# Last products of one feed-forward layer set between the first products of the next, and token sums moved to VectorE

## The chip, the cores and the metric

The program runs on one core of one Trainium2 chip. Times are device microseconds (us) from the first to the last instruction of one execution, lower is better. The core has a matrix engine (TensorE, PE in the rows; PEld is its weight load), three elementwise engines (VectorE = DVE, ScalarE = ACT, GpSimd = POOL) and SyncE (SP), whose queue issues almost every DMA here. Matmul results stand in PSUM banks, everything else in SBUF, tensors in DRAM.

## The reference, cut to what matters

```python
def reference(q, k, v, M_prev, z_prev, beta, moe_w_in, moe_w_out, moe2_w_in, moe2_w_out):
    attn = attention(q, k, v, M_prev, z_prev, beta)   # 4 batches, 8 heads, 576 tokens, 64 wide
    x = attn.transpose(0, 2, 1, 3).reshape(2304, 512)
    h = x @ moe_w_in                # 512 x 2048
    x = (h * cos(h)) @ moe_w_out    # 2048 x 512
    h = x @ moe2_w_in
    return (h * tanh(log1p(exp(h)))) @ moe2_w_out
```

All of it is float32 with zero tolerance for a single rounded pass, so the kernel splits each operand into a high part (the value rounded to the matmul's input format) and a low part (the rest), and makes three matmuls for each product: high by high, high by low, low by high.

## The kernel before, in words

The program has three parts, written one behind the other and laid out by a framework that orders the instructions of each engine itself; `tc.issue_after(mark)` holds what is written under it back until a marked instruction has been issued. `TURNS` is a table that says which engine makes a helper's pass: "v" is VectorE, "p" GpSimd, "a" ScalarE, and "vp" alternates.

**Attention and the first feed-forward layer.** `ffn` works on token blocks and units of the hidden width. `first(k)` makes the unit's hidden values (L422), an elementwise chain turns them into `g`, and `second(k)`, two units behind, multiplies `g` by w_out into the output banks `y` (L481). The hidden width is done in two halves; the first runs beside attention, the second (`m2`) on four blocks of 512 tokens and a last block of 256 tokens. That last block has four units, 96 matmuls of 256 columns for `first` and 96 for `second`. `fin_full` fetches a block's partial result from the first half (L503), adds it (L504) and stores the sum to `ysF` (L505).

**The second feed-forward layer** (`strassen_ffn`) uses Strassen's seven products in place of eight. It works on three token blocks of 768 tokens, eight groups for each. A group makes seven `product`s (A11, S2, A12, S3, S1, A22, S4, in this order), each of six matmuls of 384 columns (L630) into three PSUM banks. Between them stand the four `unit`s of the group before, nine matmuls of 512 columns each (L663). After a product, `add` (L644, VectorE) adds a bank to a value in SBUF; the Mish function runs on ScalarE (L648), the high part is cast on ScalarE (L125) and the low part taken by subtraction (L651, "ml"). Banks A and B are reused within a group: the product S3 goes on in the bank of S2 and can't start before the `add` that reads S2, nor A22 before the add that reads S3. A group needs the sums of the weights (`wq`, L601, from `wsD`) and of the tokens (`xc`).

**Token sums.** `strassen_x` fetches a token block's four quarters b11, b12, b21, b22 from `ysF` (`xr`, L565) and forms seven operands as high part (L571, ScalarE) and low part (L572, "x3l"): A11 = b11, t1 = b12 - b11 (L579), S2 = t2 = b22 - t1 (L579), A12 = b21, S3 = b22 - b12 (L589), S1 = t1, A22 = b21 - t2 (L594), S4 = b22. For the first block this runs while `ffn` still has its large blocks, and the operands are stored to `xsD` (L574); `load_sums` fetches them again (L609) with the first group's weights. For the second and third block it runs between the last group of the block before and the first of its own, straight into the operands.

The second layer's w_out is split piece by piece (`gc`): fetched to `wst`, two passes on ScalarE (L125, L140), two on VectorE (L141, L142), a cast and a low part (L553).

Of the kernel before, what the change touches and what calls it, by code (L numbers as in the profile page):

```python
# [9 lines left out]
F32 = mybir.dt.float32  # L10
# [4 lines left out]
ALU = mybir.AluOpType  # L15
# [11 lines left out]
AHEAD = 3  # L27
XSUM0 = 37
CONVR = 0.9
PACE1 = 1.5  # L30
# [6 lines left out]
    sc="p", ws="p", w0l="pv", w1l="vp", w2l="vp", w3l="vp", gl="p", gh="v", bh="a", mh="a",  # L37
    wh="ap", aT="av", yl="p", ml="vp", y0="v", y1="a", aD="v", y3="a", x3l="pv", x3d="v", ws4="p", ws2="a", wh2="a",
)
# [7 lines left out]
def attention_moe_moe_kernel(  # L47
# [14 lines left out]
    nc = tc.nc  # L62
    P = 128
# [4 lines left out]
    DFF = w1i.shape[1]  # L68
# [10 lines left out]
    xsH = tc.dram_tile([NP, P, NT], F32, name="xsH")  # L79
# [36 lines left out]
    def turn_of(kind, first=False):  # L116
        kind += "0" if first else ""
        n = counts.get(kind, 0)
        counts[kind] = n + 1
        return {"a": nc.scalar, "p": nc.gpsimd, "v": nc.vector}[TURNS[kind][n % len(TURNS[kind])]]  # L120
# [244 lines left out]
    marks = {}  # L365
# [35 lines left out]

    def ffn(pools, seq, weights, elem, load_x, mm2, finish, ready=lambda blk: True):

# [24 lines left out]

        def second(k):
            blk, half, f, n, fst, lst = seq[k]  # L430
            if fst:
                i = seq_blocks.index(blk)
                ys[blk] = [pools[i % len(pools)].tile([P, SM], F32, tag="y", name="y", bufs=BUFS["y"])
                           for _ in range(NC * blk[1] // SM)]
            gH, gL = gs.pop(k)
            T = blk[1]
            for a in range(n):
                tl, fa = (f + a) // 2, (f + a) % 2
                g = (gH[:, a * T:(a + 1) * T], gL[:, a * T:(a + 1) * T])
                mm2(ys[blk], g, weights[half][tl], fa, T, fst and a == 0, lst and a == n - 1)  # L440
            if lst:
                finish(blk, ys.pop(blk))

        seq_blocks = sorted({u[0] for u in seq})
        n = len(seq)
        for k in range(0, n + 2, 2):
            for j in (k, k + 1):
                if j < n:
                    nb = seq[min(j + NTL, n - 1)][0]
                    first(j)  # L450
                    if nb not in xs and ready(nb):
                        xs[nb] = load_x(nb)
                    yield "m1", j
            for j in (k - 2, k - 1):
                if 0 <= j < n:
                    second(j)
                    yield "m2", j
# [26 lines left out]
    def part(ys_, blk, i):  # L484

        t0, T = blk
        per = SM // T
        return ys_[:, i * per:(i + 1) * per, t0:t0 + T]
# [69 lines left out]
    def strassen_x(t0, out, store=False):  # L558
# [10 lines left out]
        def halves(n, x):  # L569
            d = wk.tile([P, 2, 2, TS], F32R, tag="xc" + u, name="xc", bufs=BUFS["xc" + u])  # L570
            nc.scalar.activation(d[:, 0], x, AF.Copy)  # L571
            turn_of("x3l").tensor_tensor(d[:, 1], x, d[:, 0].bitcast(F32), ALU.subtract)  # L572
            if store:
                nc.sync.dma_start(xsD[SLOT[n]], d.rearrange("p l c t -> p (l c t)").bitcast(F32))  # L574
            out[n] = d
# [12 lines left out]
        yield  # L588
        nc.gpsimd.tensor_tensor(b12, b22, b12, ALU.subtract)  # L589
        halves("S3", b12)  # L590
        yield
        halves("S1", t1)
        yield
        nc.gpsimd.tensor_tensor(b21, b21, t2, ALU.subtract)  # L594
        halves("A22", b21)
# [22 lines left out]

    def strassen_ffn(pool, wo, xs, w):

# [34 lines left out]
        def unit(k, g, half, f, last):  # L655
# [9 lines left out]
            if tl == ng - 1 and last:  # L665
                for t, b in enumerate(ys.pop((t0, half))):
# [3 lines left out]
                    nc.sync.dma_start(out[r:r + P, :], o)  # L670

        n = len(groups)
        g = {}
        for k in range(n + 1):
            if k < n:
# [7 lines left out]
                u2 = add(B, x1)  # L683
            if k > 0:
                unit(k - 1, g.pop((k - 1, 0, 0)), 0, 0, 0)
            if k < n:
# [3 lines left out]
                u3 = add(B, x1)  # L690
            if k > 0:
                unit(k - 1, g.pop((k - 1, 1, 1)), 1, 1, 0)
            if k < n:
# [6 lines left out]
                g[k, 1, 0] = act(c21, c21)  # L700
            if k > 0:
                unit(k - 1, g.pop((k - 1, 1, 0)), 0, 1, 1)
            if k < n:
# [5 lines left out]
                if groups[k][1] == ng - 2 and k + 2 < n:  # L709
# [3 lines left out]
                    with behind():  # L713
                        next(coming)
            if k > 0:
                unit(k - 1, g.pop((k - 1, 0, 1)), 1, 0, 1)
            yield k
# [60 lines left out]
    wo2, gc = strassen_weights(w2i, w2o)  # L778
    m2 = ffn(b_pools, seq2, {1: w_b}, elem_cos("bh"), load_block(xsH, xsL, True), mm2_t, fin_full)
    gx = strassen_x(0, {}, True)  # L780
    xs, w0 = {0: {}}, {}
    gl = load_sums(xs[0], w0)
    with tc.issue_after(marks["sp"]):
        i = made_c = 0
        while True:
# [11 lines left out]
            if i >= XSUM0 and i % 4 == 3:  # L797
                with tc.issue_after(marks["cos"]), tc.issue_after(last_sin[0]):
                    next(gx, None)
            if large[-2] in marks:  # L800
                drain(gx)
                with tc.issue_after(marks[large[-2]]):
                    next(gl, None)
    with tc.issue_after(marks[large[-2]]):
        drain(gl)
    with tc.issue_after(last_sin[0]):
        table = nc.scalar.preload_act_table_set("mish").ins
    with tc.issue_after(table), tc.issue_after(marks[large[-2]]):
        for k in strassen_ffn(b_pools[0], wo2, xs, w0):
            while made_c < min(2 * k + 4, DFF // P):  # L810
                with behind():
                    made_c = next(gc)
# [65 lines left out]
```

## Time and profile before

| | us |
|---|---|
| median of 3 runs (1068.15 to 1069.03) | 1068.41 |
| the profiled execution, its own time | 1070.39 |
| its span, first to last instruction | 1068.6 |
| PE busy in it (97%) | 1031.4 |
| DVE busy (52%) | 559.0 |
| ACT busy (50%) | 532.5 |
| POOL busy (39%) | 417.5 |
| granted TensorE clock, mean | 0.984 |

The shares are means over the whole span. Attention fills the first part up to about 560 us, the first layer's second half runs alone to 661, the second layer from there to the end. The stretches that the change touches are 634 to 704 us (the way from one layer to the next), 785 to 811 and 917 to 930 us (the token sums of the second and third token block).

### The profile page before, as it was taken

What the parts mean: (1) busy time and instruction counts of PE and PEld (TensorE: products, weight loads), DVE (VectorE), ACT (ScalarE), POOL (GpSimd) and SP (SyncE); (2) the same over time, 40 slices, a digit from 0 to 9 for tenths busy, and PEclk for the clock granted to TensorE, in tenths of its full rate; (3) what the DMA queues carried; (4) which work ended last, traced back from release to release, by engine and by line L of the source; (5) the groups of instructions that cost most, each with busy time, mean ns of one, the idle gap of its engine ahead of it and who ended that gap; (6) DMA issues with size and microseconds to landing.
All of it is one profiled execution on the core that took longest, in us unless ns stands there. A gap on an engine that the chain in (4) does not pass through costs nothing. (4 is left out here: it accounts for less than half of the span.)

```text
span 1068.6 us, 18074 instructions
## 1 busy us (share of the span) xinstructions
PE 1031.4 (97%) x6560; PEld 888.7 (83%) x6560; DVE 559.0 (52%) x1224; ACT 532.5 (50%) x1154; POOL 417.5 (39%) x407
## 2 busy tenths in 40 slices
PE   6988999999999999999999999899989999999998
PEld 4756778787878899998888889789878998898997
DVE  3689865555554537785756756435563222522221
ACT  5887675546464633425635656435544322442323
POOL 3379734323232324654656774212243111611111
PEclk7998999999999999999999999999989999999999
DMA  7477432423231165333688776975645344563431
GB/s 261 132 226 244 154 97 90 131 63 122 68 98 36 63 247 170 99 108 120 238 303 296 297 274 245 410 269 169 187 144 175 117 117 130 167 187 110 120 98 59
DMA packets 88712, 177.36 MB, mean 166 GB/s; under 512 B 8240, under 2 KB 29232, under 8 KB 87600
## 3 DMA queue, kind: packets, MB, share of 16 engines
q1 hardware_dynamic: 88624, 176.21, 49.8%
q8 instruction: 52, 0.85, 0.3%
q14 instruction: 36, 0.29, 0.1%
HBM read 132.40 MB, written 43.78 MB: 165 GB/s over the span
## 5 line engine op out<-in xcount | busy, mean ns | idle before, releaser
L481 PE MATMUL y<-g,w 128*128 128x256 f32 (+1 forms) x1344 | 219.8, 317 | 4.2 <-ACT aT L125 4.2
L663 PE MATMUL y<-wo,g 128*128 128x512 f32 x864 | 217.6, 394 | 0.0
L481 PEld LDWEIGHTS y<-g,w 128*128 128x128 f32 x1344 | 191.0, 190 | 29.5 <-issue 9.1
L630 PE MATMUL h<-xc,wq 128*128 128x384 f32 x1008 | 199.0, 341 | 8.7 <-DVE us L644 4.9
L422 PE MATMUL h<-xbH,w 128*128 128x256 f32 (+1 forms) x896 | 206.5, 317 | 0.0
L630 PEld LDWEIGHTS h<-xc,wq 128*128 128x128 f32 x1008 | 181.5, 190 | 19.9 <-DVE us L644 7.1
L663 PEld LDWEIGHTS y<-wo,g 128*128 128x128 f32 x864 | 162.0, 189 | 28.6
L651 POOL TENSOR_TENSOR g<-us,g 128x384 fp32r<-128x384 f32 x48 | 51.9, 1080 | 289.1 <-ACT g L125 282.1
L422 PEld LDWEIGHTS h<-xbH,w 128*128 128x128 f32 x896 | 150.9, 191 | 12.3 <-issue 0.7
L644 DVE TENSOR_TENSOR us<-h,us 128x384 f32<-128x384 f32 x120 | 66.7, 556 | 175.1 <-PE h L630 174.5
L274 POOL TENSOR_SCALAR at<-at,sm,omg 128x128 f32<-128x128 f32 (+2 forms) x144 | 102.6, 722 | 131.3 <-DVE sm L272 95.3
L394 POOL TENSOR_TENSOR g<-u,g 128x512 fp32r<-128x512 f32 x72 | 105.5, 1481 | 123.8 <-DVE g L127 45.1
L422 PE MATMUL h<-xbL,w 128*128 128x256 f32 (+1 forms) x448 | 141.0, 315 | 0.0
L422 PEld LDWEIGHTS h<-xbL,w 128*128 128x128 f32 x448 | 85.7, 191 | 5.4 <-issue 0.3
L376 ACT ACTIVATE u<-h 128x512 int32<-128x512 f32 x72 | 42.6, 594 | 93.2 <-PE h L422 84.5
L648 ACT ACTIVATE us<-us 128x384 f32<-128x384 f32 x72 | 37.7, 524 | 102.0 <-DVE us L644 99.4
L252 ACT ACTIVATE at<-at,mn 128x128 f32<-128x128 f32 (+3 forms) x128 | 71.0, 556 | 28.5 <-DVE mn L249 24.2
L142 DVE SCALAR_TENSOR_TENSOR wst<-wst 128x512 int32<-128x512 int32 x64 | 72.4, 1142 | 0.6
L377 DVE SCALAR_TENSOR_TENSOR u<-u,h 128x512 f32<-128x512 int32 x72 | 48.7, 681 | 43.5 <-ACT u L376 43.1
L306 PE MATMUL tp<-ident,at 128*128 128x128 f32 x384 | 64.1, 288 | 6.5 <-DVE xL L338 3.0
L333 PE MATMUL o<-aT,vt 128*64 128x128 f32 (+1 forms) x896 | 67.4, 276 | 2.0 <-ACT aT L125 2.0
L249 DVE CUSTOM_DVE_ANT_0 at<-sp,mask 128x128 f32<-128x128 f32 (+3 forms) x128 | 59.1, 482 | 19.4 <-PE sp L247 11.8
(99 smaller groups left out, 1289.3 us busy)
## 6 DMA issues: line engine op xcount, KB each, us to landing
wq<-wsD SPq DMA_DIRECT2D x168, 256.0 KB, 2.9
wsD<-ws SPq DMA_DIRECT2D x8, 1792.0 KB, 8.3
wst<-in_w1i_dram SPq DMA_DIRECT2D x16, 512.0 KB, 4.4
wst<-in_w1o_dram SPq DMA_DIRECT2D x16, 512.0 KB, 4.4
wst<-in_w2i_dram SPq DMA_DIRECT2D x16, 512.0 KB, 4.7
wst<-in_w2o_dram SPq DMA_DIRECT2D x16, 512.0 KB, 4.7
xsD<-xc SPq DMA_DIRECT2D x7, 768.0 KB, 4.5
xc<-xsD SPq DMA_DIRECT2D x7, 768.0 KB, 9.0
```

The lines of the kernel that those rows point to most:

```text
L142: nc.vector.scalar_tensor_tensor(lo, hi, 3, lo, ALU.logical_shift_left, ALU.bitwise_or)
L249: nc.vector.tensor_tensor_reduce(at[:, :N], sp[:, :N], mask[:, SM - q0:SM - q0 + N], SSC, 3.0e38, ALU.add, ALU.min, mn[:, j:j + 1])
L252: marks["act"] = nc.scalar.activation(at[:, :N], at[:, :N], AF.Exp, bias=mn[:, j:j + 1], scale=-1.0, accum_out=sm[:, j:j + 1]).ins
L274: turn_of("sc", b == 0).tensor_scalar(at[:, :N], at[:, :N], sm[:, j:j + 1], gates[j], ALU.mult, ALU.mult)
L306: nc.tensor.transpose(tp[:, c:c + P], at[:, c:c + P], ident)
L333: marks["pe"] = nc.tensor.matmul(o[j * D:(j + 1) * D, :n], st["vt"][:kk, c, j * D:(j + 1) * D], a, start=False, stop=c == i, skip_group_ch ...
L394: turn_of(kind).tensor_tensor(gL, g, gH.bitcast(F32), ALU.subtract)
L422: nc.tensor.matmul(h[:, a * T:(a + 1) * T], w_[:, c, f0:f0 + P], x_[c], start=m == 0, stop=m == 3 * NC - 1)
L481: nc.tensor.matmul(y[e // per][:, cols], w_[:, f, es], g_, start=fst and m == 0 and e % per == 0, stop=lst and m == 2, skip_group_check=True)
L630: nc.tensor.matmul(b, w[:, wl, c], x[:, xl, c], start=first and m == 0, stop=m == 5, skip_group_check=True)
L644: marks['v'] = nc.vector.tensor_tensor(c, b, x, ALU.add).ins
L663: nc.tensor.matmul(y[t], g[:, gl, t * P:(t + 1) * P], w_, start=tl == 0 and last == 0 and m == 0, stop=tl == ng - 1 and last == 1 and m == ...
```

## The change

It has four parts. `second` can hand its work over in a list instead of running it: the last two units of the last block (four parts of 12 matmuls) are no longer written behind `ffn`, but `strassen_ffn` takes one part out of that list wherever its group 0 has no unit of a group before (`between`). `load_sums` now starts at the loop's step 63 and is held back by the last store to `xsD`; before, by the store of block 1536 to `ysF`. In `TURNS`, all four low parts of a group are made by GpSimd ("ml": "p", before alternating with VectorE), and the token sums of the second and third block, low parts and the two differences L589 and L594, are made by VectorE alone; those of the first block keep their engines ("x3l0", "x3d0"). And the pieces of w_out are converted up to two pieces further ahead (`2 * k + 6`). Line numbers move by 1 to 15: after the change L422 is L423, L481 is L489, L630 is L638, L663 is L671, L644 is L652.

```diff
+XLOAD0 = 63
-    sc="p", ws="p", w0l="pv", w1l="vp", w2l="vp", w3l="vp", gl="p", gh="v", bh="a", mh="a",
-    wh="ap", aT="av", yl="p", ml="vp", y0="v", y1="a", aD="v", y3="a", x3l="pv", x3d="v", ws4="p", ws2="a", wh2="a",
+    wh="ap", aT="av", yl="p", ml="p", y0="v", y1="a", aD="v", y3="a", x3l="v", x3l0="pv", x3d0="p", x3d="v", ws4="p", ws2="a", wh2="a",
...
-        def second(k):
+        def second(k, parts=None):
...
-            for a in range(n):
+
+            def part(a):
                 tl, fa = (f + a) // 2, (f + a) % 2
                 g = (gH[:, a * T:(a + 1) * T], gL[:, a * T:(a + 1) * T])
                 mm2(ys[blk], g, weights[half][tl], fa, T, fst and a == 0, lst and a == n - 1)
-            if lst:
-                finish(blk, ys.pop(blk))
+                if lst and a == n - 1:
+                    finish(blk, ys.pop(blk))
+
+            for a in range(n):
+                if parts is None:
+                    part(a)
+                else:
+                    parts.append((part, a))
...
-                    second(j)
+                    second(j, tail if k >= n else None)
...
-            turn_of("x3l").tensor_tensor(d[:, 1], x, d[:, 0].bitcast(F32), ALU.subtract)
+            turn_of("x3l" + u).tensor_tensor(d[:, 1], x, d[:, 0].bitcast(F32), ALU.subtract)
             if store:
-                nc.sync.dma_start(xsD[SLOT[n]], d.rearrange("p l c t -> p (l c t)").bitcast(F32))
+                marks['xs'] = nc.sync.dma_start(xsD[SLOT[n]], d.rearrange("p l c t -> p (l c t)").bitcast(F32)).ins
...
-        nc.gpsimd.tensor_tensor(b12, b22, b12, ALU.subtract)
+        turn_of("x3d" + u).tensor_tensor(b12, b22, b12, ALU.subtract)
...
-        nc.gpsimd.tensor_tensor(b21, b21, t2, ALU.subtract)
+        turn_of("x3d" + u).tensor_tensor(b21, b21, t2, ALU.subtract)
...
+        def between(k, which, half, f, last):
+            if k > 0:
+                unit(k - 1, g.pop((k - 1, *which)), half, f, last)
+            elif fill:
+                part, a = fill.pop(0)
+                part(a)
...
-            if k > 0:
-                unit(k - 1, g.pop((k - 1, 0, 0)), 0, 0, 0)
+            between(k, (0, 0), 0, 0, 0)
...
-            if large[-2] in marks:
+            if i >= XLOAD0:
                 drain(gx)
-                with tc.issue_after(marks[large[-2]]):
+                with tc.issue_after(marks["xs"]):
                     next(gl, None)
...
-            while made_c < min(2 * k + 4, DFF // P):
+            while made_c < min(2 * k + 6, DFF // P):
```

On SP's queue, around the last store of the first block's token sums (`xc_7295` to `xsD_62`), the rows of before are these; `xbH_7203` and `xbL_7205` are the second halves of the last block's tokens for L422.

```order
L574 DMA xsD_62<-xc_7295 128x1536
L468 DMA xbL_7205<-xsL_58 128x2x256
L468 DMA xbH_7203<-xsH_57 128x2x256
...
L505 DMA ysF_60<-yp_7472 128x512
L601 DMA wq_7476<-wsD_61 128x512
L609 DMA xc_7478<-xsD_62 128x1536
L609 DMA xc_7510<-xsD_62 128x1536
L601 DMA wq_7508<-wsD_61 128x512
```

Of the change, at the same place:

```order
L582 DMA xsD_62<-xc_7295 128x1536
L617 DMA xc_7383<-xsD_62 128x1536
L617 DMA xc_7423<-xsD_62 128x1536
L609 DMA wq_7381<-wsD_61 128x512
L609 DMA wq_7421<-wsD_61 128x512
L609 DMA wq_7456<-wsD_61 128x512
L476 DMA xbH_7203<-xsH_57 128x2x256
L476 DMA xbL_7205<-xsL_58 128x2x256
```

The group's fetches stood behind the last `ysF` store of block 1536; now two `xc` and three `wq` stand right behind the `xsD` store, ahead of two of the last block's token tiles.

On PE, at the start of group 0, before: the last products of the first layer in their order (`w_4917` and `w_4921` belong to units 32 and 33, `w_4925` and `w_4929` to units 34 and 35), and between them the first products of the group.

```order
L481 MATMUL y<-g,w_4921 128x256 x2
L481 MATMUL y<-g,w_4922 128x256
L630 MATMUL h<-xc,wq 128x384 x6
L481 MATMUL y<-g,w_4925 128x256 x3
...
L481 MATMUL y<-g,w_4929 128x256 x2
L630 MATMUL h<-xc,wq 128x384 x5
L481 MATMUL y<-g,w_4929 128x256
...
L481 MATMUL y<-g,w_4930 128x256
L630 MATMUL h<-xc,wq 128x384 x13
```

Of the change, from the last first product of the layer on:

```order
L423 MATMUL h<-xbH,w_4928 128x256
L638 MATMUL h<-xc,wq 128x384 x4
L489 MATMUL y<-g,w_4917 128x256 x2
L638 MATMUL h<-xc,wq 128x384 x8
L489 MATMUL y<-g,w_4917 128x256
...
L638 MATMUL h<-xc,wq 128x384 x6
L489 MATMUL y<-g,w_4925 128x256 x2
L638 MATMUL h<-xc,wq 128x384 x6
...
L638 MATMUL h<-xc,wq 128x384 x12
L489 MATMUL y<-g,w_4929 128x256 x2
```

Two products of group 0 now come before units 32 and 33, two between their end and unit 34, two between 34 and 35.

On VectorE, in the token sums of the second block, before (`xt_8627` is t2; `wst` and `wo` rows belong to w_out's split, `us` rows are `add`s):

```order
L579 TENSOR_TENSOR xt_8627<-xr_8620,xt_8625 128x768
L572 TENSOR_TENSOR xc_8622<-xr_8614,xc_8622 128x768
L141 SCALAR_TENSOR_TENSOR wst_8353<-wst_8353 128x512
L141 SCALAR_TENSOR_TENSOR wst_8485<-wst_8485 128x512
L142 SCALAR_TENSOR_TENSOR wst_8353<-wst_8353 128x512
L142 SCALAR_TENSOR_TENSOR wst_8485<-wst_8485 128x512
L572 TENSOR_TENSOR xc_8661<-xr_8618,xc_8661 128x768
L644 TENSOR_TENSOR us_8676<-h_8654,us_8664 128x384
```

Of the change (here `xt_8639` is t2):

```order
L587 TENSOR_TENSOR xt_8639<-xr_8632,xt_8637 128x768
L597 TENSOR_TENSOR xr_8628<-xr_8632,xr_8628 128x768
L580 TENSOR_TENSOR xc_8634<-xr_8626,xc_8634 128x768
L580 TENSOR_TENSOR xc_8641<-xt_8639,xc_8641 128x768
L580 TENSOR_TENSOR xc_8661<-xr_8630,xc_8661 128x768
L652 TENSOR_TENSOR us_8676<-h_8654,us_8664 128x384
L580 TENSOR_TENSOR xc_8673<-xr_8628,xc_8673 128x768
L602 TENSOR_TENSOR xr_8630<-xr_8630,xt_8639 128x768
L580 TENSOR_TENSOR xc_8693<-xt_8637,xc_8693 128x768
L652 TENSOR_TENSOR us_8711<-h_8654,us_8664 128x384
```

Between t2 and the add of S2 (`us_8676`) VectorE has four passes in place of six, and none of them is of w_out's split; three more stand between that add and the add of S3 (`us_8711`). The difference S3 (L597) and the low parts that GpSimd made are now in this row.

## Rows read from the trace of the kernel before

**Rows 1.** The page: busy time by engine; costliest groups (busy, mean ns, idle before).

```profile
PE 1031.4 (97%) x6560; PEld 888.7 (83%) x6560; DVE 559.0 (52%) x1224; ACT 532.5 (50%) x1154; POOL 417.5 (39%) x407
...
L663 PE MATMUL y<-wo,g 128*128 128x512 f32 x864 | 217.6, 394 | 0.0
...
L651 POOL TENSOR_TENSOR g<-us,g 128x384 fp32r<-128x384 f32 x48 | 51.9, 1080 | 289.1 <-ACT g L125 282.1
```

**Rows 2.** Groups by line, 560 to 840: busy us, mean ns, idle before, releasers.

```profile
L630 PE MATMUL h<-xc,wq 128*128 128x384 f32 x423 | 85.2, 346 | 8.5 <-DVE us L644 4.9 <-DMA wq<-wsD 1.6 <-ACT us L681 1.5
...
L644 DVE TENSOR_TENSOR us<-h,us 128x384 f32<-128x384 f32 x50 | 27.8, 556 | 49.5 <-PE h L630 48.9
L142 DVE SCALAR_TENSOR_TENSOR wst<-wst 128x512 int32<-128x512 int32 x25 | 25.7, 1030 | 0.4
...
L141 DVE SCALAR_TENSOR_TENSOR wst<-wst 128x512 int32<-128x512 int32 x25 | 22.4, 899 | 6.8 <-ACT wst L140 6.7
...
L140 ACT ACTIVATE wst<-wst 128x512 int32<-128x512 uint32 x25 | 16.5, 661 | 0.0
```

**Rows 3.** Timeline of PE, 660 to 704: start, length, what, count.

```profile
661.38 5.92 PE L481 MATMUL y<-g,w 128*128 128x256 f32 x48
...
702.02 2.27 PE L630 MATMUL h<-xc,wq 128*128 128x384 f32 x12
```

**Rows 4.** Chain of work that ended last, 940 to 950: start, length.

```profile
941.69 2.10 PE h L630 x12
943.79 2.08 PE y L663 x9
```

**Rows 5.** Timeline of all engines, 785 to 812; in brackets idle before, releaser.

```profile
785.64 2.27 PE L630 MATMUL h<-xc,wq 128*128 128x384 f32 x12
...
787.60 0.96 DVE L579 TENSOR_TENSOR xt<-xr,xt 128x768 f32<-128x768 f32 x1 [0.60 <-DMA xr<-ysF]
...
787.75 4.28 PE L663 MATMUL y<-wo,g 128*128 128x512 f32 x18
...
788.47 1.78 DVE L572 TENSOR_TENSOR xc<-xr,xc 128x768 fp32r<-128x768 f32 x1
...
789.40 2.56 POOL L589 TENSOR_TENSOR xr<-xr 128x768 f32<-128x768 f32 x1
...
790.17 4.56 DVE L141 SCALAR_TENSOR_TENSOR wst<-wst 128x512 int32<-128x512 int32 x2
...
791.92 2.26 POOL L572 TENSOR_TENSOR xc<-xt,xc 128x768 fp32r<-128x768 f32 x1
...
795.86 0.95 DVE L572 TENSOR_TENSOR xc<-xr,xc 128x768 fp32r<-128x768 f32 x1
...
797.33 4.21 PE L630 MATMUL h<-xc,wq 128*128 128x384 f32 x12 [4.23 <-DVE us L644]
...
811.04 1.31 PE L663 MATMUL y<-wo,g 128*128 128x512 f32 x5
```

**Rows 6.** Windows: length, busy PE PEld DVE ACT POOL, clock, DMA share, GB/s.

```profile
798.00:800.00 2.00, 2.00 (x8) 2.00 (x7) 2.00 (x2) 1.13 (x4) 2.00 (x2) 0.50 0.00 0
634.00:644.00 10.00, 10.00 (x47) 8.30 (x46) 5.26 (x7) 4.84 (x7) 6.91 (x7) 1.00 0.70 221
664.00:704.00 40.00, 35.77 (x199) 31.98 (x198) 17.26 (x25) 15.60 (x29) 10.02 (x7) 0.96 1.02 398
```

**Rows 7.** Timeline of all engines, 917 to 931.

```profile
919.42 1.03 DVE L579 TENSOR_TENSOR xt<-xr,xt 128x768 f32<-128x768 f32 x1 [0.66 <-DMA xr<-ysF]
...
920.12 4.28 PE L663 MATMUL y<-wo,g 128*128 128x512 f32 x18
...
926.78 2.36 PE L630 MATMUL h<-xc,wq 128*128 128x384 f32 x12 [0.27 <-ACT us L648]
```

**Rows 8.** Timeline of SP's queue, 630 to 675: DMA issues.

```profile
634.56 0.32 SPq L574 DMA_DIRECT2D xsD<-xc  x1
...
660.33 0.43 SPq L601 DMA_DIRECT2D wq<-wsD  x1
```

More of the change, by code (lines that the diff above doesn't have):

```diff
@@ L400, in units, with ffn @@
         return [(blk, half, f, n) for f in range(0, NFH, n)]
-    def ffn(pools, seq, weights, elem, load_x, mm2, finish, ready=lambda blk: True):
+    def ffn(pools, seq, weights, elem, load_x, mm2, finish, ready=lambda blk: True, tail=None):
         xs = {}
@@ L617, in behind, with strassen_ffn @@
         return es
-    def strassen_ffn(pool, wo, xs, w):
+    def strassen_ffn(pool, wo, xs, w, fill):
         ng = DFF // (2 * P)
@@ L690, in strassen_ffn @@
                 u3 = add(B, x1)
-            if k > 0:
-                unit(k - 1, g.pop((k - 1, 1, 1)), 1, 1, 0)
+            between(k, (1, 1), 1, 1, 0)
             if k < n:
@@ L700, in strassen_ffn @@
                 g[k, 1, 0] = act(c21, c21)
-            if k > 0:
-                unit(k - 1, g.pop((k - 1, 1, 0)), 0, 1, 1)
+            between(k, (1, 0), 0, 1, 1)
             if k < n:
@@ L714, in strassen_ffn @@
                         next(coming)
-            if k > 0:
-                unit(k - 1, g.pop((k - 1, 0, 1)), 1, 0, 1)
+            between(k, (0, 1), 1, 0, 1)
             yield k
@@ L778, in attention_moe_moe_kernel @@
     wo2, gc = strassen_weights(w2i, w2o)
-    m2 = ffn(b_pools, seq2, {1: w_b}, elem_cos("bh"), load_block(xsH, xsL, True), mm2_t, fin_full)
+    fill = []
+    m2 = ffn(b_pools, seq2, {1: w_b}, elem_cos("bh"), load_block(xsH, xsL, True), mm2_t, fin_full, tail=fill)
     gx = strassen_x(0, {}, True)
@@ L799, in attention_moe_moe_kernel @@
                     next(gx, None)
-            if large[-2] in marks:
+            if i >= XLOAD0:
                 drain(gx)
-                with tc.issue_after(marks[large[-2]]):
+                with tc.issue_after(marks["xs"]):
                     next(gl, None)
-    with tc.issue_after(marks[large[-2]]):
+    with tc.issue_after(marks["xs"]):
         drain(gl)
@@ L807, in attention_moe_moe_kernel @@
         table = nc.scalar.preload_act_table_set("mish").ins
-    with tc.issue_after(table), tc.issue_after(marks[large[-2]]):
-        for k in strassen_ffn(b_pools[0], wo2, xs, w0):
-            while made_c < min(2 * k + 4, DFF // P):
+    with tc.issue_after(table), tc.issue_after(marks["xs"]):
+        for k in strassen_ffn(b_pools[0], wo2, xs, w0, fill):
+            while made_c < min(2 * k + 6, DFF // P):
                 with behind():
```

## The prediction

> **What bounds the kernel now.** I read the busy times first. PE is busy for 1031.4 us of the span, and no matmul of L663 ever finds PE idle [rows 1]: the second layer is bound by TensorE, and what the change can win lies only where PE stands still or runs slowly. So I looked for those places in the groups by line, then in PE's timeline, and last in the timeline of all engines around each.
>
> Between 560 and 840 us PE idles 8.5 us ahead of L630: 4.9 for VectorE's add, 1.6 for weight loads, 1.5 for ScalarE's copy [rows 2]. To see what a stretch loses I price its matmuls as they run where nothing waits: in the chain that ended last, 12 of L630 take 2.10 us (0.175 each) and 9 of L663 take 2.08 (0.231) [rows 4]; 48 of L481 with 256 columns take 5.92 (0.123) [rows 3].
>
> Transition from layer to layer, 661.38 to 702.02, 40.64 us [rows 3]: 96 of L481 (11.8), 66 of L630 (11.55) and 45 of L663 (10.4) make 33.8. Lost: 6.9.
>
> Second token block, 785.64 to 811.04, 25.40 us [rows 5]: 54 of L630 (9.45) and 39 of L663 (9.0) make 18.5. Lost: 6.9. Of that 4.23 is one wait of PE for the add of S2. The 12 matmuls behind it take 4.21 in place of 2.10 [rows 5]; the granted clock there is 0.50, its lower level, after PE had stood idle [rows 6]. So a gap of 4 us cost almost 3 us more in slow matmuls.
>
> Third token block: 0.27 us of wait [rows 7], so 0.3. The three stretches lose 14.1 us together.
>
> **The change part by part.** No matmul, elementwise pass or DMA is added or taken away; all terms are waits that go or come.
>
> *Transition: the fetches.* Before, the group's first weights are issued at 660.33, 26 us after the last store of the token sums at 634.56 [rows 8], into a stretch where the DMA engines are full (share 1.02, 398 GB/s). Around the store they are at 0.70 and 221 GB/s [rows 6]. Now two token sums (768 KB each by their shapes) and three weights (256 KB each) stand behind the store. They and the store (768 KB) and the two token tiles behind them (256 KB each) are 3.7 MB; at 398 GB/s that is 9.2 us, so the tiles land near 644. The layer's first products want them when 48 of the last 96 are done: 661.4 less 5.9 for the other 48, less 5.6 for the 24 second products of 512 columns that stand between (0.231 each), is 649.9. I cost the fetches at nothing, with 6 us of cover; if the queues run at 221 GB/s the tiles land at 651 and PE is 1 us late. The waits for weights and sums in this stretch (1.6 [rows 2], and 0.5 at the first product) go.
>
> *Transition: the parts between products.* Group 0 had no units of a group before to fill its waits for adds; 48 matmuls of L481 now fill them. The copy's wait of 1.5 goes as well, since w_out's four passes ahead of it on ScalarE are made a group earlier. What is late next: in group 1, S3 waits for the add of S2, and on VectorE four passes of w_out's split and one add of the last block stand ahead of it. From the end of S4 of group 0: add and Mish 1.35, two ScalarE passes of 0.661 to 2.65, then on VectorE 2 x (0.899 + 1.030) [rows 2] and 0.7 (a 512-column add, an estimate from 0.556 at 384 columns) to 7.2, and the add 0.56: 7.7. PE has 7 of L481, three products and 9 of L663 in the meantime, 6.1 us. I keep 1.6 us of loss; it would be near 0 if the passes of the split ran with GpSimd quiet.
>
> *Token sums on VectorE alone.* The price of a pass decides. A pass of 768 elements took 0.96 and 0.95 us where GpSimd was idle or nearly so (787.60, 795.86), and 1.78 beside GpSimd (788.47). Two passes L141, 0.899 each in the mean [rows 2], took 4.56 us while GpSimd ran a difference of 2.56 and a low part of 2.26 [rows 5]. So the passes on the two engines lengthened each other; GpSimd now has in this stretch only the low parts of `g`, 1.08 each [rows 1]. I take 0.96, and add 0.82 (1.78 - 0.96) for each low part that falls on a pass, one in each of two chains per block.
>
> Second block: t2 starts at 787.60, and VectorE makes five passes (t2, S3's difference, three low parts) and the add, 0.56: 787.60 + 4.80 + 0.56 = 792.96. S3 is wanted after the 18 matmuls from 787.75 [rows 5] and the product A12: 787.75 + 4.16 + 1.05 = 792.96. No wait, or 0.82 with a low part. Then three passes and an add, 3.44, against two products, 2.10: A22 is 1.34 late, 2.16 with a low part. Loss 3.0 (1.3 without overlap). In general, for a pass of p us the block loses 8p - 6.34.
>
> Third block, the same chain from 919.42: the add ends at 924.78; S3 is wanted at 920.12 [rows 7] + 5.21 = 925.33. With the overlaps 0.27 and 2.16: loss 2.4 (0.8 without); in general 8p - 6.89.
>
> The Trainium skill, SBUF — State Buffer, section Who interferes with whom, says that a VectorE instruction with two SBUF inputs and a GpSimd instruction that reads SBUF share a port pair as an exclusive lock, so that the later one waits out the earlier. The trace agrees: the two L141 ended at 794.73, about one pass behind the end of GpSimd's 2.26 at 794.18. By that rule a low part would hold a pass for up to its whole 1.08 in place of 0.82, and the sum would be 1062.3; it speaks against giving GpSimd more low parts.
>
> *Low parts on GpSimd in all other groups.* I cost them at nothing: half of them run there already at 1.08 and L663 never waits [rows 1]. Without that cover each late one costs PE directly (rival 3).
>
> *Sum.* Before 14.1, after 1.6 + 3.0 + 2.4 = 7.0: a gain of 7.1. Against the profiled execution's own time, 1070.39 (1.8 above its span), that is 1063.3; the median of the runs stands 2.0 lower, so 1068.4 - 7.1 = **1061.3**. Without overlaps the losses are 3.7: 1058.0, and with nothing lost in the transition 1056.4. On the other side p = 1.2 with no further overlap gives 3.3 + 2.7 + 1.6 = 7.6, 1061.9, and p = 1.4 gives 10.8, 1065.1.
>
> **The rivals.**
> 1. VectorE's passes stay slow (slower side). Eight passes in one row with adds between them that PE waits for: if each takes 1.78 as at 788.47, the blocks lose 7.9 + 7.4, with the transition 16.9, and about 2.7 more for each block in which the clock falls again: 1071 to 1077. It decides from p = 1.61 on. For it: 1.78 is measured in just this stretch, and the row of work on VectorE grows. Against it: GpSimd's 2.26 and 2.56 passes, beside which 1.78 was seen, are gone. Chance 0.05; half of it (p from 1.2 to 1.5, 1062 to 1067) 0.13.
> 2. The transition stays late: the last units' elementwise chain, which had a unit's worth of other work to hide in, ends some 1 to 2 us before its use by my order of events, and the last block's tiles wait behind five fetches. Each us late costs one: with 2 to 5 us back, 1063 to 1066. Chance 0.10.
> 3. The low parts on GpSimd hold L663 in every group: 0.33 us in each of the 22 groups besides eats the gain; at 0.5 it is 1065. Against it the 0.0 of L663 [rows 1]. Chance 0.04.
> 4. Nothing changes: the fetches waited only for bandwidth that is used up anyway and the blocks trade one wait for another of the same length, 1068. Chance 0.04.
>
> **How the numbers follow.** The forecast has 0.64; its own range, from the bounds above, is 1056.4 to 1063.5. The range for 8 in 10 takes in rival 2 and the partial form of rival 1: 1056 to 1066.5. A measurement of this kernel can tell 0.2% (2.1 us) from no change. Faster by more than that, below 1066.3: forecast 0.64, most of the partial rivals (0.11 and 0.09) and of rival 3 (0.02), 0.86. Within it: 0.06. Slower: 0.05 from rival 1 and 0.03 from the others, 0.08.
>
> **What the profile after would show.** The fetch rows of group 0 stand near 635 on SP; no PE wait for `wq` or `xc` near 667 to 688; L481 between products up to about 685. At both token blocks the wait for S2's add is under 1 us and one for S3's add, ahead of A22, is 1.3 to 2.2; the 768-element passes are 0.96, with some 1.8; the clock stays at 1.00. Wrong would make it: a mean of the passes near 1.6, PE waits ahead of L663 (now L671), or a wait on L423 near 650 for the token tiles.

## The result, and the profile after

The changed kernel takes 1055.44 us in the median (1054.89 to 1058.53), the kernel before 1068.28 in the same runs: ratio 0.9882, 95% interval [0.9866, 0.9899], 12.6 us less (10.8 to 14.3). The forecast of 1061.3 had the direction and the places, and little more than half of the gain; the time lies 0.6 us below the range. Of the changed kernel's profiled execution the span is 1053.8.

The page's busy times and the group of the second layer's first products, which answer to [rows 1, 2], the group over the whole span:

```profile
PE 1024.1 (97%) x6560; PEld 884.5 (84%) x6560; DVE 536.4 (51%) x1187; ACT 531.6 (50%) x1154; POOL 439.7 (42%) x444
...
L671 PE MATMUL y<-wo,g 128*128 128x512 f32 x864 | 218.9, 393 | 0.0
L638 PE MATMUL h<-xc,wq 128*128 128x384 f32 x1008 | 198.2, 337 | 0.8 <-ACT us L656 0.5 <-DVE us L652 0.3
```

PE's idle time ahead of these products is 0.8 us, where the stretch from 560 to 840 us alone had 8.5. The units (L671) still never find PE idle, although GpSimd now makes all low parts.

The way between the layers, PE's timeline (start, length, what, count; in brackets the wait and who ended it), which answers to [rows 3]:

```profile
659.29 0.86 PE L638 MATMUL h<-xc,wq 128*128 128x384 f32 x4
...
661.62 5.67 PE L489 MATMUL y<-g,w 128*128 128x256 f32 x46
...
679.11 2.24 PE L671 MATMUL y<-wo,g 128*128 128x512 f32 x9
681.19 2.27 PE L638 MATMUL h<-xc,wq 128*128 128x384 f32 x12
683.75 1.33 PE L638 MATMUL h<-xc,wq 128*128 128x384 f32 x6 [0.29 <-DVE us L652]
684.92 7.03 PE L671 MATMUL y<-wo,g 128*128 128x512 f32 x30
691.79 0.51 PE L638 MATMUL h<-xc,wq 128*128 128x384 f32 x2
```

One wait of 0.29 us is left of five. By 691.79 PE has done 96 of L489, 66 of L638 and 39 of L671, 32.4 us at the prices of [rows 3, 4], in 32.5. SP's queue and the windows (length, busy PE PEld DVE ACT POOL, granted clock, DMA share, GB/s) answer to [rows 6, 8]:

```profile
632.46 0.32 SPq L582 DMA_DIRECT2D xsD<-xc  x1
632.83 1.38 SPq L617 DMA_DIRECT2D xc<-xsD  x2
634.26 1.69 SPq L609 DMA_DIRECT2D wq<-wsD  x3
635.99 0.45 SPq L476 DMA_DIRECT2D xbH<-xsH  x1
```

```profile
634.00:644.00 10.00, 10.00 (x53) 8.53 (x52) 6.02 (x8) 5.45 (x8) 6.08 (x7) 1.00 1.03 373
664.00:704.00 40.00, 39.71 (x231) 36.58 (x230) 24.63 (x32) 23.64 (x46) 20.29 (x15) 1.00 0.89 318
```

The fetches are issued some 27 us sooner (632.83, before 660.33), fill the DMA engines there (share 1.03 at 634 to 644) and leave room later (0.89 in place of 1.02). No matmul of L423 waits, so the tiles behind the five fetches were in time.

The second token block, all engines, which answers to [rows 5]:

```profile
775.89 2.57 POOL L659 TENSOR_TENSOR g<-us,g 128x384 fp32r<-128x384 f32 x2 [2.16 <-ACT g L126]
...
776.92 2.27 PE L638 MATMUL h<-xc,wq 128*128 128x384 f32 x12
777.67 1.60 DVE L587 TENSOR_TENSOR xt<-xr,xt 128x768 f32<-128x768 f32 x1 [1.21 <-DMA xr<-ysF]
...
779.03 4.28 PE L671 MATMUL y<-wo,g 128*128 128x512 f32 x18
779.20 0.94 DVE L597 TENSOR_TENSOR xr<-xr 128x768 f32<-128x768 f32 x1
...
780.07 0.94 DVE L580 TENSOR_TENSOR xc<-xr,xc 128x768 fp32r<-128x768 f32 x1
...
782.67 0.54 DVE L652 TENSOR_TENSOR us<-h,us 128x384 f32<-128x384 f32 x1
...
783.15 2.27 PE L638 MATMUL h<-xc,wq 128*128 128x384 f32 x12
...
785.69 2.40 PE L638 MATMUL h<-xc,wq 128*128 128x384 f32 x12 [0.27 <-ACT us L656]
786.17 0.55 DVE L652 TENSOR_TENSOR us<-h,us 128x384 f32<-128x384 f32 x1
```

The add of S2 ends at 783.21 (782.67 + 0.54), and S3, the second half of the 12 matmuls from 783.15, is wanted at 784.20: 0.99 us early, where the forecast had it on time or 0.82 late. The add of S3 ends at 786.72 and A22, the second half of the 12 from 785.69, is wanted at 786.74: just in time. The only wait is 0.27 for the Mish of bank A. Note how the rows of one engine overlap: a pass is 0.94 long, but the next starts 0.87 behind its start. In the third block, too, 0.27 us of wait for ScalarE's Mish is all there is, as in [rows 7]:

```profile
911.84 2.40 PE L638 MATMUL h<-xc,wq 128*128 128x384 f32 x12 [0.27 <-ACT us L656]
```

### The profile page after: what moved, and what is told of

The parts are those of the page before. It is cut to its first block, busy times and chain, and to the rows that moved or that the text cites. A ratio compares the mean times of both kernels' runs of the same rounds, so it can differ in the third digit from the quotient of the medians.

```text
span 1053.8 us, 18081 instructions
## 1 busy us (share of the span) xinstructions
PE 1024.1 (97%) x6560; PEld 884.5 (84%) x6560; DVE 536.4 (51%) x1187; ACT 531.6 (50%) x1154; POOL 439.7 (42%) x444
## 4 chain that ended last, share of the span: by engine, by line
PE 90%; ACT 3%; DVE 2%; DMA 2%; issue 1%; POOL 1%; SPq 0%; ACTq 0%; DVEq 0%; POOLq 0%
PE h L423 20%; PE y L489 20%; PE y L671 19%; PE h L638 16%; PE o L334 5%; PE tp L307 4%; PE sp L248 3%; PE o L323 2%; PE mp L287 2%; PE sp L261 1%; ACT at L253 1%; DMA wst<-in_w1o_dram 1%; POOL at L275 1%; DVE wst L142 1%; DMA qt<-in_qp_dram 0%
## 5 line engine op out<-in xcount | busy, mean ns | idle before, releaser
L489 PE MATMUL y<-g,w 128*128 128x256 f32 (+1 forms) x1344 | 220.7, 317 | 4.2 <-ACT aT L126 4.2
L671 PE MATMUL y<-wo,g 128*128 128x512 f32 x864 | 218.9, 393 | 0.0
L489 PEld LDWEIGHTS y<-g,w 128*128 128x128 f32 x1344 | 191.2, 190 | 29.3 <-issue 9.1
L423 PE MATMUL h<-xbH,w 128*128 128x256 f32 (+1 forms) x896 | 206.3, 316 | 0.0
L659 POOL TENSOR_TENSOR g<-us,g 128x384 fp32r<-128x384 f32 x96 | 100.9, 1053 | 252.1 <-ACT g L126 208.1
L638 PE MATMUL h<-xc,wq 128*128 128x384 f32 x1008 | 198.2, 337 | 0.8 <-ACT us L656 0.5
L652 DVE TENSOR_TENSOR us<-h,us 128x384 f32<-128x384 f32 x120 | 66.7, 556 | 242.3 <-PE h L638 241.8
L638 PEld LDWEIGHTS h<-xc,wq 128*128 128x128 f32 x1008 | 179.2, 188 | 12.5 <-ACT us L656 1.2
L671 PEld LDWEIGHTS y<-wo,g 128*128 128x128 f32 x864 | 160.7, 188 | 26.9
L423 PEld LDWEIGHTS h<-xbH,w 128*128 128x128 f32 x896 | 150.6, 190 | 12.6 <-issue 0.7
L423 PE MATMUL h<-xbL,w 128*128 128x256 f32 (+1 forms) x448 | 140.8, 314 | 0.0
L423 PEld LDWEIGHTS h<-xbL,w 128*128 128x128 f32 x448 | 85.4, 191 | 5.3 <-issue 0.3
```

What stands on the lines that cost most here:

```text
L423: nc.tensor.matmul(h[:, a * T:(a + 1) * T], w_[:, c, f0:f0 + P], x_[c], start=m == 0, stop=m == 3 * NC - 1)
L489: nc.tensor.matmul(y[e // per][:, cols], w_[:, f, es], g_, start=fst and m == 0 and e % per == 0, stop=lst and m == 2, skip_group_check=True)
L638: nc.tensor.matmul(b, w[:, wl, c], x[:, xl, c], start=first and m == 0, stop=m == 5, skip_group_check=True)
L652: marks['v'] = nc.vector.tensor_tensor(c, b, x, ALU.add).ins
L659: ins = turn_of("ml").tensor_tensor(g[:, 1], dst, g[:, 0].bitcast(F32), ALU.subtract).ins
L671: nc.tensor.matmul(y[t], g[:, gl, t * P:(t + 1) * P], w_, start=tl == 0 and last == 0 and m == 0, stop=tl == ng - 1 and last == 1 and m == ...
```

## The experiments

The runs of a kernel are compared with runs of the kernel before on the same chip, whose median was 1068.46, 1070.36 and 1069.48 us for the three sets of four below; so the ratio is what to compare, and "us less" is the ratio on 1068.3. "Way" is PE's idle time between the layers, "second" and "third" that in the token blocks, from the waits of PE in the one profile of each kernel; matmuls that run slowly behind a wait come on top.

| kernel | ratio [95%] | us less | way | second | third |
|---|---|---|---|---|---|
| before | 1 | 0 | 4.2 | 4.2 | 0.3 |
| the change | 0.9882 [0.9866, 0.9899] | 12.6 | 0.3 | 0.3 | 0.3 |
| sums alone | 1.0012 [0.9998, 1.0026] | -1.3 | 6.4 | 1.5 | 0 |
| fetch, hand-over and pace | 0.9892 [0.9875, 0.9908] | 11.5 | 0.3 | 0.9 | 0.3 |
| change with pace 4 | 0.9920 [0.9906, 0.9935] | 8.5 | 0.2 | 2.4 | 0.3 |
| change, differences on GpSimd | 0.9889 [0.9871, 0.9907] | 11.9 | 0.3 | 0.2 | 0.3 |
| pace alone | 0.9943 [0.9922, 0.9965] | 6.1 | 3.9 | 0.8 | 2.6 |
| change without hand-over | 0.9926 [0.9903, 0.9949] | 7.9 | 3.9 | 0.4 | 0.3 |
| change with the late fetch | 0.9978 [0.9965, 0.9991] | 2.4 | 6.2 | 0.3 | 0.3 |
| change, three more passes | 0.9889 [0.9866, 0.9913] | 11.9 | 0.3 | 0.4 | 0.6 |
| fetch alone | 0.9963 [0.9948, 0.9977] | 4.0 | 2.9 | 2.3 | 1.0 |
| fetch and pace | 0.9943 [0.9928, 0.9959] | 6.1 | 4.0 | 0.8 | 0.3 |
| fetch and hand-over | 0.9913 [0.9897, 0.9929] | 9.3 | 0.2 | 3.3 | 0.7 |
| change, low parts alternate | 0.9885 [0.9867, 0.9903] | 12.3 | 0.3 | 0.3 | 0.2 |

After the result two theories stood against each other. Theory A: what made VectorE late in the second block were the passes of w_out's split in its row, so the pace does it, and who makes the token sums matters little. Theory B: what made it late was GpSimd's share of the sums beside it, so the move does it.

**Sums alone.** The kernel before, with the token sums' line of the table as in the change, and with the three `turn_of` lines that read it (not shown here):

```diff
-    wh="ap", aT="av", yl="p", ml="vp", y0="v", y1="a", aD="v", y3="a", x3l="pv", x3d="v", ws4="p", ws2="a", wh2="a",
+    wh="ap", aT="av", yl="p", ml="vp", y0="v", y1="a", aD="v", y3="a", x3l="v", x3l0="pv", x3d0="p", x3d="v", ws4="p", ws2="a", wh2="a",
```

> Only the token sums of the second and third block move to VectorE; the transition, the low parts and the pace of w_out's split stay as before, so four split passes still stand in VectorE's row between t2 and the add of S2. Theory A (the split's passes in that row and the transition are what cost): the transition keeps its 6.9 us, the second block loses about 4 in place of 6.9, so 1064.5 to 1066. Theory B (GpSimd beside VectorE is what cost, the move removes it): the second block loses under 1 us, so 1061 to 1062.5.

No gain at all. The second block does improve, to 1.5 us of wait, but the framework ordered the way between the layers anew as well, and there PE now waits longer, as PE's timeline shows:

```profile
690.86 8.08 PE L663 MATMUL y<-wo,g 128*128 128x512 f32 x24 [4.49 <-ACT wo L125]
...
797.29 2.35 PE L630 MATMUL h<-xc,wq 128*128 128x384 f32 x12 [1.49 <-DVE us L644]
```

As a time it tells the theories apart badly, since two things moved; it fits neither number.

**Fetch, hand-over and pace**, the opposite half. The change with the table of before:

```diff
-    ... ml="p", ... x3l="v", ...
+    ... ml="vp", ... x3l="vp", ...
-        turn_of("x3d" + u).tensor_tensor(b12, b22, b12, ALU.subtract)
+        nc.gpsimd.tensor_tensor(b12, b22, b12, ALU.subtract)
```

(and the same for the other difference). "vp" in place of the "pv" of before gives the second and third block the turns that they had: the first block's seven passes are no longer counted with them.

> The opposite half: the transition and the earlier split of w_out as in the change, token sums and low parts shared with GpSimd as before. Theory A: nearly the whole gain is here, 1055 to 1058, with no wait of PE over 1 us at 785. Theory B: the blocks lose what they lost before, 6.9 and 0.3, so 1061 to 1063, with a wait of some 4 us for the add of S2.

Nearly the whole gain is here; as the whole cause, Theory B falls. VectorE and GpSimd do hold each other up, as all engines' timeline in the second block shows:

```profile
778.33 2.57 POOL L597 TENSOR_TENSOR xr<-xr 128x768 f32<-128x768 f32 x1
...
779.11 5.13 DVE L580 TENSOR_TENSOR xc<-xr,xc 128x768 fp32r<-128x768 f32 x2
...
780.87 2.56 POOL L580 TENSOR_TENSOR xc<-xt,xc 128x768 fp32r<-128x768 f32 x1
...
784.16 0.55 DVE L652 TENSOR_TENSOR us<-h,us 128x384 f32<-128x384 f32 x1
...
784.76 2.36 PE L638 MATMUL h<-xc,wq 128*128 128x384 f32 x12 [0.56 <-DVE us L652]
```

From t2's start (778.17) to the end of the add it is 6.5 us in place of the change's 5.5. But that lies almost within the room there is: PE waits 0.56.

**The change with pace 4.**

```diff
-            while made_c < min(2 * k + 6, DFF // P):
+            while made_c < min(2 * k + 4, DFF // P):
```

> The change with the pace of w_out's split set back, so that four split passes of about 0.66 us from start to start stand between t2 and the add of S2 of the second block, and one of L561 ahead of the add of S3. Theory A: the add of S2 comes 2.6 us later than in the change, where it was 1.0 early: S3 waits 1.6, A22 some 2 more, 1059 to 1062. Theory B: VectorE has room, 1055 to 1057.

4.1 us of the gain go, as Theory A had it. The split's passes stand between t2 and the add, and PE waits for it, then runs slowly:

```profile
779.01 0.96 DVE L587 TENSOR_TENSOR xt<-xr,xt 128x768 f32<-128x768 f32 x1 [1.83 <-DMA xr<-ysF]
...
782.45 1.28 DVE L142 SCALAR_TENSOR_TENSOR wst<-wst 128x512 int32<-128x512 int32 x2
...
783.66 0.68 DVE L143 SCALAR_TENSOR_TENSOR wst<-wst 128x512 int32<-128x512 int32 x1
...
786.60 0.55 DVE L652 TENSOR_TENSOR us<-h,us 128x384 f32<-128x384 f32 x1
...
787.20 3.77 PE L638 MATMUL h<-xc,wq 128*128 128x384 f32 x12 [2.42 <-DVE us L652]
```

From t2 to the add's end it is 8.1 us, though every pass of the sums is VectorE's. In the table the second block goes by the pace first: with pace 6 it waits 0.2 to 0.9 us whoever makes the sums. With pace 4 the engine counts too: 1.5 and 2.4 us where VectorE makes them, 2.3 to 4.2 where they are shared.

**The change with the differences on GpSimd.** Both `turn_of("x3d" + u)` are `nc.gpsimd` again.

> The change with only the two differences for S3 and A22 of the second and third block given back to GpSimd. VectorE's row to the add of S2 loses one pass of 0.87, and GpSimd's pass of 1.8 to 2.6 runs beside it. Theory A (an overlap costs about what the pass saved): within 1 us of the change, 1055 to 1056.5. Theory B (each overlap holds VectorE for the length of GpSimd's pass): both adds 2 us later in each block, 1057.5 to 1060.

Within the noise of the change, as Theory A had it. One pass shows what an overlap costs:

```profile
778.66 2.57 POOL L597 TENSOR_TENSOR xr<-xr 128x768 f32<-128x768 f32 x1
...
779.44 2.61 DVE L580 TENSOR_TENSOR xc<-xr,xc 128x768 fp32r<-128x768 f32 x1
```

VectorE's pass ends at 782.05, 0.82 after GpSimd's at 781.23: so it waited GpSimd's out and then took about its usual time.

**Pace alone.** The kernel before with `2 * k + 6`.

> The kernel before with one number changed: w_out's split runs up to six pieces ahead in place of four. It takes the split's four passes out of VectorE's row in the second block, and earlier in the transition; the token sums stay shared with GpSimd. Theory A (these passes are the second block's 6.9 us, not GpSimd's share of the sums): the block loses about 1, so 1061 to 1063. Theory B (the scheduler only pushes the same passes into the transition, which then loses more): 1065 to 1069.

6.1 us less, within the 5.3 to 7.3 that Theory A's times mean against 1068.3; the second block's wait falls to 0.8, with the sums shared as before. The way stays at 3.9: PE now waits 1.9 us for ScalarE's copy of x1 (L696 in the change; it reads A11's bank, in which A12 goes on). The third block waits 2.6 in place of 0.3, 1.5 of it for this copy.

**The change without hand-over.**

```diff
-                    second(j, tail if k >= n else None)
+                    second(j)
```

> The change without handing over: units 34 and 35 are written behind the first layer again; the early fetch stays. Theory A (the early fetch does it, the framework had put these matmuls between group 0's products anyway): 0 to 1 us on the change, 1055 to 1056.8. Theory B (group 0 needs the parts as cover for its adds): some three waits of 0.5 to 1 us come back, 1057 to 1059.

4.7 us of the gain go, about 1 more than Theory B had, which the intervals don't tell apart, and in another place: not small waits for adds in group 0, but one of 3.9 us for the copy of x1 in group 1.

```profile
689.35 1.35 PE L638 MATMUL h<-xc,wq 128*128 128x384 f32 x6 [3.94 <-ACT us L696]
```

**The change with the late fetch.**

```diff
-            if i >= XLOAD0:
+            if large[-2] in marks:
...
-                with tc.issue_after(marks["xs"]):
+                with tc.issue_after(marks[large[-2]]):
```

(the same mark at the two places behind it).

> The change with the first group's sums fetched behind block 1536's last store again. Theory A: the waits for weights and sums of the transition come back, 2.0 us, and those of ScalarE and VectorE behind them partly: 1057.5 to 1060. Theory B (the parts between the products cover the fetches): 1055 to 1056.5.

10.2 us of the gain go, far more than the 2.0 of the waits for weights. These came back at their size (2.2), but PE then waits 3.4 us for the copy of x1 too. Slow matmuls behind the waits do the rest, as PE's timeline and the windows show (columns as above):

```profile
690.49 1.51 PE L638 MATMUL h<-xc,wq 128*128 128x384 f32 x6 [3.38 <-ACT us L696]
```

```profile
690.00:700.00 10.00, 9.12 (x37) 7.61 (x38) 6.39 (x9) 4.41 (x9) 5.33 (x4) 0.83 1.05 398
```

The granted clock is 0.83 here where the change has 1.00. From the last first product at 660.25 to 703.98, in PE's timeline, the matmuls are worth 34.7 us at the prices of [rows 3, 4]: 9.0 lost, 6.2 of them as waits, 2.8 as slow matmuls. The change loses 0.1 on the same way, so 8.9 of the 9.9 us by which the two profiled executions differ (1063.7 against 1053.8) lie here.

**The change with three more passes.**

```diff
             turn_of("x3l" + u).tensor_tensor(d[:, 1], x, d[:, 0].bitcast(F32), ALU.subtract)
+            if n == "A11" and not store:
+                for _ in range(3):
+                    nc.vector.tensor_tensor(d[:, 1], x, d[:, 0].bitcast(F32), ALU.subtract)
```

> The change with A11's low part of the second and third block made four times over (the same values), three more VectorE passes of 0.87 from start to start: one ahead of the add of S2, one between it and the add of S3, one behind. Theory A (the row stands just in time: 1.0 us ahead of S3, nothing ahead of A22): S3 doesn't wait, A22 waits 1.2 to 1.5 in each block, so 1057.5 to 1059. Theory B (VectorE has room): 1055 to 1056.5.

Theory A fails here on its number: 0.7 us by the ratio, inside the noise. The add of S3 does come later, 9.7 us behind t2's start in place of 9.1, but the framework, which lays out the passes too, put six matmuls of a unit ahead of A22 (the six from 789.58):

```profile
783.86 3.86 PE L641 MATMUL h<-xc,wq 128*128 128x384 f32 x18
788.10 1.64 PE L674 MATMUL y<-wo,g 128*128 128x512 f32 x6 [0.38 <-ACT g L126]
...
789.58 1.23 PE L641 MATMUL h<-xc,wq 128*128 128x384 f32 x6
```

So VectorE has more room than the order of the change shows, as long as the framework foresees the passes.

The last four runs take the way between the layers apart, with the engines of before. **Fetch alone** is the change with the table, the pace and the `second(j)` of before; **fetch and pace** has the pace of 6 besides, **fetch and hand-over** the hand-over at pace 4.

> The kernel before with the early fetch alone: no hand-over, pace 4, engines as before. ScalarE's row now has six split passes ahead of the copy of x1 in group 1 (four before). Theory A (the fetch only shifts the wait: weights come in time, the copy waits about 1 us longer, the second block stays at 6.9): 1065 to 1068. Theory B (the early fetch is the core of the gain): 1058 to 1062.

> The kernel before with the early fetch and the pace of 6: no hand-over, engines as before. Eight split passes stand ahead of the copy in group 1. Theory A: the copy makes PE wait about 4 us and the clock falls behind it, the second block is under 1: 1061 to 1063.5. Theory B (the parts as cover are worth nothing): 1056 to 1058.

> The kernel before with the early fetch and the hand-over, pace 4, engines as before. Four split passes ahead of the copy, with the parts as cover. Theory A: the transition loses under 1 us, the second block what it lost before, 6.9: 1061 to 1063. Theory B (the second block's loss depends on the sums, and without the pace the transition is late too): 1064 to 1068.

In PE's timeline, of fetch alone, of fetch and pace, and of fetch and hand-over:

```profile
687.50 1.31 PE L638 MATMUL h<-xc,wq 128*128 128x384 f32 x6 [2.88 <-ACT us L696]
791.66 3.85 PE L638 MATMUL h<-xc,wq 128*128 128x384 f32 x12 [2.26 <-DVE us L652]
```

```profile
687.87 2.17 PE L638 MATMUL h<-xc,wq 128*128 128x384 f32 x6 [4.01 <-ACT us L696]
```

```profile
786.80 2.35 PE L638 MATMUL h<-xc,wq 128*128 128x384 f32 x12 [2.24 <-DVE us L652]
```

Fetch alone takes the waits for weights away, and the copy's grows from 1.50 to 2.88: 4.0 us less in sum, above Theory A and short of B. Fetch and pace gains no more than the pace alone: the second block is gone, but the copy waits 4.0, as Theory A had it. Fetch and hand-over has no wait worth the name on the way and keeps the second block's, 3.3 us; at 9.3 it did better than either theory said, in part since the matmuls behind its 2.24 us of waiting ran at full speed (12 in 2.35). ScalarE's timeline in fetch and pace shows what the copy waits for:

```profile
682.89 0.66 ACT L126 ACTIVATE wst<-wst 128x512 f32<-128x512 f32 x1
...
686.77 0.69 ACT L141 ACTIVATE wst<-wst 128x512 int32<-128x512 uint32 x1
687.33 0.48 ACT L696 ACTIVATE us<-h 128x384 f32<-128x384 f32 x1
```

Eight split passes, 0.55 us apart, run one behind another from 682.89, and the copy that PE waits for comes last. In the change only four stand there, and they start sooner:

```profile
678.53 0.65 ACT L126 ACTIVATE wst<-wst 128x512 f32<-128x512 f32 x1
...
681.18 0.47 ACT L696 ACTIVATE us<-h 128x384 f32<-128x384 f32 x1
```

The number of split passes ahead of the copy in ScalarE's row is 4 with the fetch and the hand-over at either pace, 6 with the fetch alone, 8 with the fetch and pace 6: the wait is 0, 2.9 and 4.0 us. (Before it is 6 too, and the wait only 1.50, since PE itself comes later there, by its waits for weights.) So the parts handed over do more than fill group 0's waits: where the fetch is early too, the framework puts the copy ahead of half the passes. With the hand-over and the late fetch it stays behind six, and PE waits 3.4 (690.49 above); neither part does it alone.

**The change with alternating low parts.** `ml="vp"`.

> The change with the low parts of g alternating between VectorE and GpSimd again. Theory A (both engines have room in the groups, and in the token sums a low part on VectorE costs 0.46 where one on GpSimd costs 0.66): as the change, within 0.2 %. Theory B (the low parts stand in VectorE's row ahead of the adds): 1057 to 1060.

Theory A: no difference that can be seen. Low parts on GpSimd neither help nor harm within the noise.

**The second block in all profiles.** VectorE's row from t2's start to the end of the add of S2 tells the pace and the engine apart, wherever the block stands:

| token sums | pace | row, us | kernels |
|---|---|---|---|
| shared | 4 | 9.7 | before; fetch alone; fetch and hand-over |
| VectorE | 4 | 8.1 | sums alone; change with pace 4 |
| shared | 6 | 6.5 to 7.3 | pace alone; fetch and pace; fetch, hand-over and pace |
| VectorE | 6 | 4.9 to 5.5 | the change, also without hand-over, with the late fetch, with alternating low parts |

With the differences alone on GpSimd it is 6.0, with three more passes 5.8. So the pace is worth 2.4 to 3.2 us of the row and the engine 1.0 to 2.4. PE's wait follows from it: add the time by which t2 starts behind A11, from -0.1 to 2.3 us in these profiles, and PE waits for what goes beyond 7.4. In the eight kernels that wait for this add the sum less the wait is 7.4 (before: 1.96 + 9.68 - 4.23); in the other six the sum is 6.2 to 7.3, and there is no such wait.

## Why the prediction was right in direction and short in size

What held. PE is the bound and its waits are the gain: 14.1 us lost before, 0.8 of waits left after, a difference of 13.3 against 12.6 measured. The fetches cost nothing, the waits for weights went, no rival came true: the passes took 0.94 (1.60 for t2 beside a low part), the tiles and the last units' chain were in time, and L671 never waits.

What failed are three terms of "after 1.6 + 3.0 + 2.4 = 7.0"; they measured 0.29, 0.27 and 0.27, and the two of 0.27 are waits for a Mish that the blocks' terms did not hold: of the waits for adds that they priced, none came. Even the best case, "with nothing lost in the transition", left 2.1 us in the blocks, so its 1056.4 was no floor.

The 1.6 of the transition was built on "2 x (0.899 + 1.030)" [rows 2], means over 560 to 840 us in which passes beside GpSimd weigh. In their place VectorE's row in the changed kernel has 0.6 to 0.85 from start to start, 3.4 us for the five instructions priced at 4.6. The prediction named this way out, "near 0 if the passes of the split ran with GpSimd quiet"; only one low part (681.36 to 682.68) ran beside them:

```profile
679.76 0.69 DVE L142 SCALAR_TENSOR_TENSOR wst<-wst 128x512 int32<-128x512 int32 x1 [1.70 <-ACT wst L141]
680.49 0.69 DVE L143 SCALAR_TENSOR_TENSOR wst<-wst 128x512 int32<-128x512 int32 x1
...
683.15 0.55 DVE L652 TENSOR_TENSOR us<-h,us 128x384 f32<-128x384 f32 x1
```

The five passes and "three passes and an add" of the blocks erred in two steps. First, "I take 0.96" is a pass's length, while the next starts 0.87 after it; [rows 5] showed that too, 787.60 to 788.47. From t2's start to the end of S2's add it is 5.54 us in the change, 1.60 of t2 beside a low part included, against 6.18 priced with one. The third block's is 5.53 (903.74 to 909.27). The low part priced into each block's second chain fell on no pass: from the add of S2 to that of S3 it is 3.51 and 3.60, against 4.26. Second, "t2 starts at 787.60" took over the start from one execution. t2 waits for the fetched quarters, and they land at another moment in each profile: t2 begins 1.96 us after A11's start before (787.60 - 785.64) and 0.75 after it in the change (777.67 - 776.92). The two, 0.64 and 1.21, turn the 0.82 late into 0.99 early (the other 0.04 is PE's, 5.17 for 5.21), and that lead covers most of what was priced for A22. The third block went the same way: 1.08 early in place of 0.27 late.

Not in the numbers but in the cause, the prediction said too little: it put the gain of the blocks down to token sums on VectorE alone. In the row up to the add the pace is worth more than the engine, as the table above shows. In time the move to VectorE is worth nothing that can be told from 0: 1.1 us on top of the rest (12.6 against 11.5, intervals overlapping), -0.8 at pace 4 (8.5 against 9.3), -1.3 alone. The pace is worth 6.1 alone, 4.1 in the change, and 2.1 and 2.2 on top of the fetch and of fetch and hand-over, these two with overlapping intervals. The row of before already held it: the 4.56 us of two L141 in [rows 5] are the split's. What it said of ScalarE, "the copy's wait of 1.5 goes as well", came true, but not by the cause it gave: an earlier split alone made that wait longer (1.9, and 4.0 with the early fetch), and only the hand-over together with the early fetch removed it. Six of the split's passes stood ahead of the copy before, not four.

Three smaller slips changed no forecast. Rival 1 holds against itself that the passes beside which 1.78 was seen are gone; but that pass, from 788.47 to 790.25, began beside a low part of `g`, which the change keeps, and ended 0.81 behind it:

```profile
788.34 1.10 POOL L651 TENSOR_TENSOR g<-us,g 128x384 fp32r<-128x384 f32 x1 [5.93 <-ACT g L125]
```

In rival 3, 1065 belongs to half of 0.33 us a group; 0.5 in 22 groups is 11 us, 1072.3. And 1063.5, the upper end of the forecast's own range, is the result of none of its sums.

What stays open is how far the lead of t2 in the change is its own doing; in part it is luck. In twelve of the fourteen profiles the second block's four fetches are issued within some 2 us, and t2 began 7.5 to 9.0 us after the first, for no reason that the runs show; the change has the shortest time. In fetch alone and in fetch and hand-over the fetches are issued over 4.6 and 7.5 us, t2 began 12.9 and 15.7 us after the first, and it waited for none. The gain hangs little on it: without the hand-over t2 began 2.29 us behind A11, later than before, and with a row of 4.90 PE still did not wait for the add of S2.

## What to carry to other kernels

Price a row of passes by the distance from start to start at that place in the row, not by the length of one or a mean over a stretch with other neighbours. Where an engine's result is late, list everything that stands ahead of it in that engine's row, and move first the work that nobody waits for soon: here one number of the pace did more than another engine for five passes. Parts of a change that cover each other's waits are worth more together than alone (the fetch 4.0 and the pace 6.1 alone, 6.1 for the two, 11.5 with the hand-over), so single ablations do not add up.

## What the runs showed of the hardware

VectorE and GpSimd, at elementwise work with two inputs, did not run slower side by side, they took turns: VectorE's pass beside a GpSimd pass ended 0.82 us after it (782.05 against 781.23), 0.81 after it in the kernel before (790.25 against 789.44), and in the run with fetch, hand-over and pace two passes took 5.13 us beside two of GpSimd. This is what the Trainium skill says in SBUF — State Buffer, section Who interferes with whom: a VectorE instruction with two SBUF inputs and a GpSimd instruction that reads SBUF exclude each other for a whole instruction. The trace agrees, by these ends. The contended price of 1.78 that the prediction used is thus no price of a pass but whatever was left of the other's.

TensorE's granted clock did not fall by the length of a wait alone. After 2.26 us of waiting in fetch alone twelve matmuls took 3.85 us in place of 2.10, at a granted clock of 0.52 (the lower level, 1.2 GHz, for nearly all of 792 to 795); after 2.42 in the change with pace 4 they took 3.77, at 0.53. After 2.24 in fetch and hand-over they took 2.35, at 1.00. What else decides it the runs do not show. So some 1.7 us of the difference between these kernels come from the clock and not from the length of the wait.
